# GpSimd waits for VectorE operations on two SBUF inputs, more time for the first loads in the event model, and other seeds for the order

## The chip, the cores and the metric

The kernel runs on one core of one Trainium2 chip. The metric is device time in microseconds (us) of one execution. Two kernels are compared by the medians of several runs; a single further execution is taken with the hardware profiler, and all rows of the profile come from that one.

The core has five engines that run their own instruction streams and meet at semaphores: TensorE (PE in the profile; its weight loads are shown apart as PEld), VectorE (DVE), ScalarE (ACT), GpSimd (POOL) and SyncE (SP), which here issues nearly all DMAs. Each engine takes its instructions strictly in the order in which the program wrote them.

## The reference, cut to what matters

The kernel computes a block and all of its gradients: out = g · A(x) + (1 − g) · B(x), with 2048 rows of 512 columns in bf16.

```
qkv = (x @ wqkv)                    # 32 heads of 16 columns
scores = q @ k.T * 16 ** -0.5       # masked: 0 <= i - j < 256
a = softmax(scores) @ v @ wo        # A: attention in a sliding window of 256
gate = x @ W_gate; up = x @ W_up    # 512 -> 1376
b = (relu(gate) * up) @ W_down      # B
g = sigmoid((x * gate_w).sum(-1))
out = g * a + (1 - g) * b
_out, _vjp = jax.vjp(f, x, wqkv, wo, W_gate, W_up, W_down, gate_w)
return (_out, *_vjp(grad_out))
```

So there are eight outputs: the block's output, and the gradients of x, wqkv, wo, W_gate, W_up, W_down and gate_w.

## The kernel before

**Tiles and stages.** Attention is cut into 32 stages of four heads by 512 rows. A stage has score products (S) and products of the output gradient with V (dP), both made by the matmuls of line L1101 in a "row" mode, in which four matmuls with 16 or 32 rows of weights share the array. ScalarE takes the exponential of S out of PSUM (L1144), GpSimd masks the triangles at the edges of the window (L1122), and VectorE multiplies the masked result by dP (L1149). The sums over keys and queries are matmuls of line L1165 in a "col" mode, with 32 columns of weights each. Everything else on TensorE is "dense": projections, feed-forward layers and weight gradients go through one helper (L698), the products that give the output and the gradient of x through another (L1472).

**The feed-forward layer.** `front` handles one of eleven chunks of 128 hidden columns. For every 512 rows it makes three products by matmul, takes a relu on ScalarE or VectorE (L936, L938), then multiplies on VectorE (L941, L945). Two more products have both inputs in SBUF (L948); they may go to GpSimd or to VectorE. A chunk's results go to DRAM by a DMA and come back transposed.

**The order of the work.** No loop of the program issues instructions directly. The program first lists operations (`op`, `dma`), each with the engines that may run it, a cost in nanoseconds for each, a rank, and the buffers it reads and writes. Then `Flow.run` walks through a small event model: whenever an engine of the model is free, it takes the ready operation with the lowest rank, emits its instructions, and marks the engine as taken for the stated cost. So the model's costs fix both the order within each engine's stream and which engine gets an operation that two could run. On the chip the order is kept, and semaphores do the waiting; the model's times are not enforced.

**Lock operations.** Operations that may run on VectorE with their inputs in SBUF alone carry `lock=True`: L948, the products U and pr of a stage (L1196, L1198), the copies at L1034 and L1036, the scaling of the output gradient by the gate (L877), and in the last part the small sums of `dzf` (L1572, L1573, L1607, L1608) and the running sum of `gate_sum` (L1540). In the model VectorE starts such an operation only while GpSimd is free, and GpSimd starts nothing until it has ended (`locked`). That rule lives in the model alone: the emitted program has no semaphore for it.

**DMAs in the model.** All DMAs that SP and ACT issue share one line of time (`dma_free`), with a cost by bytes. An operation that would start a DMA of rank 3 or more is held back while that line is over 1500 ns ahead. `load_first` brings the first rows and weights, and `load_rows` then loads the other rows of x and of the output gradient, three loads of 512 KB each. The first stage of attention needs the arrays `QD_d` and `KV_d`, which the first projections write to DRAM (L838), and reads them back (L1024 to L1026).

**Seeds.** Among dense matmul operations the rank gets a small pseudo-random addition. Its seed and its size come from the list `SEEDS`, one entry for every 20,000 ns (`STRETCH`) of the model's time, and the last entry holds for all that follows:

```python
s_ = SEEDS[min(int(now / STRETCH), len(SEEDS) - 1)]
return o.rank + SPREADS[s_ % len(SPREADS)] * mix(s_ // len(SPREADS), o.seq)
```

TensorE's mode counts in the model too: changing between row, col and dense costs 97 ns (`SWITCH`), and an addition of 2.5 to the rank (`HOLD`) puts off a change from dense to col for up to 800 ns. When TensorE has nothing to do and has lately been idle, the model inserts a matmul into a free bank (L1638) that nobody reads.

**The last part.** After the attention stages come the products of L1472 for the output and the gradient of x. There `final` adds, on GpSimd, two partial results that come back from DRAM (L1577, L1582), and stores them.

Of the kernel before, what the change touches and what calls it, by code (L numbers as in the profile page):

```python
# [34 lines left out]
def place(segs, dist):  # L35
# [13 lines left out]
PE, DVE, ACTE, POOL, SP = "PE", "DVE", "ACT", "POOL", "SP"  # L49
START = 20000  # L50
LATENCY = {PE: 230, DVE: 135, ACTE: 165, POOL: 100, SP: 2300}
# [2 lines left out]
HOLD, WAIT = 2.5, 800  # L54
SPREADS, STRETCH = (0.05, 0.15, 0.02, 0.4), 20000
SEEDS = (
# [3 lines left out]
)  # L60
SPAN, LOW, NEED, PHASE = 3413.3, 3000, 3600, 0

# [154 lines left out]
class Flow:  # L217
# [6 lines left out]

    def __init__(self):
        self.ops, self.spare, self.fill, self.filled = [], None, None, 0

    def op(self, times, fn, r=(), w=(), order=(), deps=(), keep=(), rank=5, mode="", nbytes=0, heavy=False,
           lead=0, lock=False):
# [45 lines left out]
    def run(self):  # L275
        events, count = [], 0
        ready = {e: [] for e in LATENCY}
        free = {e: 0.0 for e in LATENCY}
        now, dma_free, pool_free, locked, mode, heavy, done = 0.0, 0.0, 0.0, 0.0, "", False, 0
        self.log, self.busy, self.slow, ran = [], [], {}, {}  # L280

# [42 lines left out]
        while done < len(self.ops):  # L324
            progress = True
            while progress:
                progress = False
                for e in (PE, ACTE, DVE, POOL, SP):
# [24 lines left out]
                    else:  # L353
                        o = min(cands, key=lambda o: (o.rank, o.seq))
# [6 lines left out]
                    if e == PE:  # L361
                        took = ahead(now + SWITCH * (o.mode != mode), took)
                        if o.mode != mode:
                            took += SWITCH
                        mode = o.mode
                        if o.mode == "den":
                            heavy = o.heavy
                    o.fn(e)
                    o.state = 1
                    self.log.append((now, took, e, o))  # L370
                    free[e] = now + took
# [40 lines left out]
def kernel(  # L412
# [41 lines left out]
    WARM = 4  # L454
    MASKV = {DVE: 410, ACTE: 710}
    DTT = 640
    TT = 425
    KR = 2.5
    HQ, OUTS, DIRECT = (SP,), 2, 3
# [197 lines left out]
        rings[nm].ordered = True  # L657

    fl = Flow()
    op = fl.op  # L660
    EN = {PE: nc.tensor, ACTE: nc.scalar, DVE: nc.vector, POOL: nc.gpsimd, SP: nc.sync}

# [79 lines left out]
    def load_rows(dst, src_d, sb, on=(SP,)):  # L742
        dma(lambda q: q.dma_start(dst[:, 4 * sb:4 * sb + 4, :],
                                  src_d[sb * W:(sb + 1) * W, :].rearrange("(t p) d -> p t d", p=P)),
            w=[(dst, sb)], nbytes=512 * KB, rank=2 if on == by_pool else 3, on=on)

    def load_first():

# [918 lines left out]
```

## Time and profile before

| what | value |
|---|---|
| median of 3 runs | 802.11 us (800.44 to 804.85) |
| profiled execution: its own time | 803.82 us |
| profiled execution: span of its instructions | 802.1 us |
| mean granted TensorE clock | 0.998 |
| bytes read from HBM, written to it | 55.02 MB, 55.74 MB |

The span runs from the first to the last instruction in the trace; about 1.7 us of the execution's own time lie around it. How to read rows of the groups: the line in the program, the engine, the operation, what it writes and reads, the shape, the count; behind the bar the busy time in us and the mean duration of one in ns; behind the second bar the idle time of the engine just before, and whose end released it. Busy intervals of successive instructions on an engine overlap a little, since one begins while the one before drains.

### The profile page before, as it was taken

The page shows a single profiled execution, that of the slowest core. Times are in us where ns is not written, and L with a number is a line of the kernel's source. Part 1 is how long each engine was busy: PE and PEld are TensorE (multiplying, and loading weights), DVE is VectorE, ACT ScalarE, POOL GpSimd, SP SyncE. Part 2 cuts the span into 40 slices and gives each one's busy share as a digit, 9 for nine tenths or more (in the row PEclk, how much of TensorE's full clock was granted, in tenths as well). Part 3 has the DMA queues.
Part 4 walks back from the last instruction along what each step waited for, and adds up shares of the span by engine and source line. Part 5 has one row for each costly group of instructions (what it writes and reads, how often), then busy time and mean ns, then how long its engine had stood idle before and what let it go on. Part 6 is the DMA issues. An engine that isn't in the chain of part 4 may idle for free.

```text
span 802.1 us, 24151 instructions
## 1 busy us (share of the span) xinstructions
PE 782.5 (98%) x8842; PEld 371.0 (46%) x8950; DVE 696.6 (87%) x1239; ACT 589.1 (73%) x1183; POOL 546.8 (68%) x972
## 2 busy tenths in 40 slices
PE   8899999999999999999999999999999999999999
PEld 5443444445445454444454554544443434344444
DVE  3589999999999999999999988998999999933573
ACT  4786889888888778887888998888877888421121
POOL 2497879787797988797988676776766666222145
PEclk9999999999999999999999999999999999999999
DMA  9879657478679999997899979686745685497896
GB/s 239 183 178 222 154 135 185 113 175 181 130 189 163 233 178 188 231 208 220 189 202 210 212 157 204 161 193 182 221 108 173 160 246 173 141 272 223 230 236 191
DMA packets 313009, 152.18 MB, mean 190 GB/s; under 512 B 203161, under 2 KB 303194, under 8 KB 312250
## 3 DMA queue, kind: packets, MB, share of 16 engines
q1 hardware_dynamic: 311314, 148.53, 77.0%
q0 software_dynamic: 496, 1.44, 0.9%
q8 instruction: 70, 1.15, 0.6%
q10 hardware_dynamic: 1080, 0.66, 0.3%
q14 instruction: 49, 0.40, 0.2%
HBM read 55.02 MB, written 55.74 MB: 138 GB/s over the span
## 4 chain that ended last, share of the span: by engine, by line
PE 91%; DMA 3%; issue 2%; DVE 2%; ACT 1%; SPq 1%; ACTq 0%; DVEq 0%
PE banks L698 42%; PE banks L1472 21%; PE banks L1101 15%; PE banks L1165 10%; DMA arena<-in_A_x_dram 1%; DVE arena L1149 1%; PE banks L1200 1%; ACT arena L1144 1%; DMA arena<-QD_d 1%; DMA arena<-HD_d 1%; PE banks L802 1%; DMA arena<-wt_d 0%; PE banks L1638 0%; SPq L1006 0%; SPq L768 0%
## 5 line engine op out<-in xcount | busy, mean ns | idle before, releaser
L1149 DVE TENSOR_TENSOR arena<-arena,banks 128x512 bf16<-128x512 bf16 (+1 forms) x740 | 455.8, 665 | 20.5 <-PE banks L1101 12.8
L1144 ACT ACTIVATE arena<-banks 128x512 bf16<-128x512 f32 (+1 forms) x740 | 394.3, 588 | 80.3 <-PE banks L1101 61.0
L1122 POOL TENSOR_SCALAR_AFFINE_SELECT arena<-arena 128x256 bf16<-128x256 bf16 (+1 forms) x752 | 345.4, 483 | 142.6 <-ACT arena L1144 132.8
L698 PE MATMUL banks<-arena 128*128 128x512 bf16 (+4 forms) x1929 | 385.5, 334 | 5.5 <-issue 1.6
L698 PEld LDWEIGHTS <-arena 128*128 128x128 bf16 (+1 forms) x2000 | 175.1, 98 | 154.9 <-issue 54.5
L1472 PE MATMUL banks<-arena 128*128 128x512 bf16 (+1 forms) x747 | 181.8, 380 | 3.2 <-issue 1.9
L1101 PE MATMUL banks<-arena 32*128 32x128 bf16 (+5 forms) x2944 | 155.8, 271 | 5.5 <-DMA arena<-QD_d 2.0
L1101 PEld LDWEIGHTS <-arena 32*128 32x128 bf16 (+1 forms) x2944 | 47.9, 92 | 140.3 <-issue 136.3
L1472 PEld LDWEIGHTS <-arena 128*128 128x128 bf16 (+1 forms) x784 | 69.6, 98 | 89.8 <-issue 17.4
L676 ACT CAST arena<-banks 128x512 bf16<-128x512 f32 (+4 forms) x150 | 71.4, 489 | 44.9 <-PE banks L698 35.2
L1165 PE MATMUL banks<-arena 128*32 128x128 bf16 (+5 forms) x2944 | 92.2, 271 | 0.4 <-DVE arena L1149 0.2
L948 POOL TENSOR_TENSOR arena<-arena 128x512 bf16<-128x512 bf16 (+1 forms) x73 | 84.1, 1156 | 3.4 <-ACT arena L676 2.1
L1165 PEld LDWEIGHTS <-arena 128*32 128x32 bf16 (+1 forms) x2944 | 61.2, 95 | 30.8 <-issue 18.2
L1196 POOL TENSOR_TENSOR arena<-arena 128x512 bf16<-128x512 f32 x31 | 35.9, 1158 | 16.1 <-issue 12.4
L1576 ACT ACTIVATE arena<-banks,g_all 128x512 f32<-128x512 f32 x12 | 8.2, 687 | 42.8 <-PE banks L1472 28.4
L678 DVE CAST arena<-banks 128x512 bf16<-128x512 f32 (+3 forms) x50 | 31.0, 625 | 9.5 <-PE banks L698 7.2
L1577 POOL TENSOR_TENSOR arena<-arena 128x512 bf16<-128x512 f32 x12 | 15.3, 1276 | 29.5 <-ACT arena L1576 12.1
L1198 POOL TENSOR_TENSOR arena<-arena 128x512 bf16<-128x512 bf16 x29 | 33.4, 1153 | 0.8 <-DVE arena L1196 0.7
L1582 POOL TENSOR_TENSOR arena<-arena 128x512 bf16<-128x512 f32 x12 | 15.2, 1265 | 25.9 <-DMA arena<-dx_p 14.4
L941 DVE SCALAR_TENSOR_TENSOR arena<-arena,banks 128x512 bf16<-128x512 bf16 (+1 forms) x44 | 29.9, 679 | 0.6 <-PE banks L698 0.2
L945 DVE TENSOR_TENSOR arena<-arena,banks 128x512 bf16<-128x512 bf16 (+1 forms) x44 | 29.8, 676 | 0.0
L1567 DVE SCALAR_TENSOR_TENSOR arena<-banks,g_all,arena 128x512 bf16<-128x512 f32 x12 | 8.8, 748 | 23.6 <-ACT arena L1576 23.6
(95 smaller groups left out, 421.6 us busy)
## 6 DMA issues: line engine op xcount, KB each, us to landing
ffn_d<-arena SPq DMA_DIRECT2D x40, 384.0 KB
arena<-ffn_d SPq DMA_DIRECT2D x88, 128.0 KB
out_dram<-arena SPq DMA_DIRECT2D x66, 128.0 KB
arena<-HD_d SPq DMA_DIRECT2D x32, 256.0 KB
KV_d<-arena SPq DMA_DIRECT2D x32, 128.0 KB
QD_d<-arena SPq DMA_DIRECT2D x32, 128.0 KB
arena<-KV_d SPq DMA_DIRECT2D x32, 128.0 KB
arena<-QD_d SPq DMA_DIRECT2D x32, 128.0 KB
```

The lines of the kernel that those rows point to most:

```text
L676: nc.scalar.copy(out, in_)
L678: EN[e].tensor_copy(out, in_)
L698: return lambda start, stop: nc.tensor.matmul(out_fn(), lhsT=lhs_fn(), rhs=rhs_fn(), start=start, stop=stop)
L948: op({POOL: t_pool(W, 2), DVE: TT}, lambda e, q=q, k=k, b=b: EN[e].tensor_tensor(out=q["act"][:fs, k, :], in0=q["dhs"][:fs, :], in1=q[b][: ...
L1101: nc.tensor.matmul(bank, lhsT=lt[rs, ls], rhs=rt[rs, rsl], start=True, stop=True)
L1122: nc.gpsimd.affine_select(out=v, in_=v, compare_op=ALU.is_ge, fill=0.0, base=0 if kind == "D" else -1, pattern=[[0, 2], [0, cnt], [sgn, P] ...
L1144: op({ACTE: t_act(u.width)}, lambda e, u=u, b=b, bank_=bank_: nc.scalar.activation(part(u, u.Pt, b), bank_[:, :u.width], ACT.Exp), r=[bank ...
L1149: op({DVE: t_dve(u.width)}, lambda e, u=u, b=b, bank_=bank_: nc.vector.tensor_tensor(out=part(u, u.Pd, b), in0=part(u, u.Pt, b), in1=bank_ ...
L1165: nc.tensor.matmul(acc[32 * i:32 * i + wt.shape[1], q0:q0 + cnt * P], lhsT=wt, rhs=m[:, i % 2, col * P:(col + cnt) * P], start=(k == 0), s ...
L1196: op({POOL: t_pool(W, 2), DVE: t_dve(W)}, lambda e: EN[e].tensor_tensor(out=U[:], in0=ri[:], in1=qd[:], op=ALU.mult), r=[ri, qd], w=[U], r ...
L1198: op({POOL: t_pool(W, 2), DVE: TT}, lambda e: EN[e].tensor_tensor(out=pr[:], in0=OB[:, half], in1=U[:], op=ALU.mult), r=[(OB, half), U], w ...
L1472: nc.tensor.matmul(bank[:], lhsT=l_(), rhs=r_(), start=(lo + k == 0), stop=(lo + k == n - 1))
```

## The change

Three things are changed.

1. A real dependency. When the model emits a lock operation on VectorE, its last instruction is remembered. The next operation emitted for GpSimd that is no DMA gets a semaphore dependency on it: its first instruction waits until the VectorE instruction has ended. One GpSimd operation per remembered instruction waits; if two lock operations come before it, it waits for the later one. The costs in the model stay as they are.
2. The model's account of the start. SP and ScalarE are taken as busy for the first 800 ns, and the six loads of `load_rows` count as 1.2 times their bytes in the model. The transfers themselves are the same.
3. Other seeds. The 40 entries of `SEEDS` are replaced by 41 others. Both lists end in 0.

```diff
 SEEDS = (
-    16914, 36512, 34193, 28631, 17467, 29116, 12171, 23200, 15639, 5432, 22622, 33577, 13710, 2535, 15625, 10269,
...
-    33217, 31493, 2658, 18911, 29376, 22502, 20490, 0,
+    27601, 11357, 7558, 39987, 14011, 590, 1533, 1815, 15419, 11593, 7005, 28378, 21291, 5427, 32748, 20263,
...
+    23287, 31690, 18602, 19721, 10719, 36758, 32196, 39551, 0,
 )
...
+        self.held, self.traced, self.after = None, None, None
...
-        free = {e: 0.0 for e in LATENCY}
+        free = {e: 800.0 if e in (SP, ACTE) else 0.0 for e in LATENCY}
...
+                    made = self.traced()
+                    count_ = len(made)
                     o.fn(e)
+                    made = [i for i in made[count_:]]
+                    if e == DVE and o.lock:
+                        self.held = made[-1]
+                    elif e == POOL and self.held is not None and not o.nbytes:
+                        self.after(made[0], self.held)
+                        self.held = None
...
+    EARLY_X = 1.2
...
+    def after(inst, first):
+        tc.add_manual_dep(inst, first.name, mybir.DependencyInfo(mybir.DependencyClass.Sync, mybir.DependencyReason.DATA), reason="port")
+
+    fl.traced, fl.after = lambda: nc.cur_bb.bb.instructions, after
...
-            w=[(dst, sb)], nbytes=512 * KB, rank=2 if on == by_pool else 3, on=on)
+            w=[(dst, sb)], nbytes=EARLY_X * 512 * KB, rank=2 if on == by_pool else 3, on=on)
```

Since the whole stream comes out of one walk through the model, items 2 and 3 can alter the order of nearly every instruction and the engine of every operation that has a choice. The amount of arithmetic stays the same.

2 rows, old and new, of the table SEEDS are left out of this document.

## The prediction

> **What bounds the kernel now.** The page comes first: span, busy times, and the chain that ended last.
>
> ```profile
> span 802.1 us, 24151 instructions
> PE 782.5 (98%) x8842; PEld 371.0 (46%) x8950; DVE 696.6 (87%) x1239; ACT 589.1 (73%) x1183; POOL 546.8 (68%) x972
> PE 91%; DMA 3%; issue 2%; DVE 2%; ACT 1%; SPq 1%; ACTq 0%; DVEq 0%
> ```
>
> TensorE is busy for 98% of the span and is 91% of the chain. All its idle time is 802.1 − 782.5 = 19.6 us. That is the most that removing visible waits can win, so the next view asks where it lies: busy times of four stretches (start, first attention stage, middle, last part).
>
> ```profile
> 0.00:32.00 32.00, 26.02 (x273) 17.51 (x278) 14.03 (x41) 16.93 (x33) 8.51 (x24) 0.99 0.97 236
> 32.00:40.00 8.00, 7.95 (x57) 3.52 (x55) 5.25 (x8) 6.05 (x14) 5.28 (x14) 0.81 0.44 110
> 40.00:700.00 660.00, 648.32 (x8007) 303.45 (x8100) 628.04 (x1079) 547.05 (x1095) 501.22 (x910) 1.00 0.78 182
> 700.00:802.10 102.10, 100.25 (x512) 46.49 (x519) 49.30 (x114) 19.06 (x43) 31.80 (x25) 1.00 0.85 230
> ```
>
> The columns are length, then busy time of PE, PEld, DVE, ACT and POOL, granted clock, DMA share, GB/s. TensorE idles 6.0 us before 32 us, 11.7 us between 40 and 700 us, and 1.9 us after that. The granted clock falls to 0.81 between 32 and 40 us. VectorE is nearly full in the middle as well (628 of 660 us), so what it loses there is not easily made up; GpSimd has 159 us left.
>
> The waits then say who is late (us in total, times, longest); all engines first, then TensorE's own.
>
> ```profile
> PEld L1101 <- issue: 136.3, 375, 2.4
> POOL arena L1122 <- ACT arena L1144: 132.8, 181, 9.2
> PEld L698 <- issue: 54.5, 255, 0.7
> PEld L1165 <- issue: 18.2, 72, 0.4
> PEld L1472 <- issue: 17.4, 83, 0.2
> ```
> ```profile
> PE banks L1101 <- DMA arena<-QD_d: 2.0, 1, 2.0
> PE banks L698 <- DVE arena L1149: 0.9, 2, 0.7
> PE banks L1101 <- DVE arena L1149: 0.5, 2, 0.3
> ```
>
> Two things are to be seen. TensorE's named waits are few: one DMA in front (2.0 us), and VectorE's L1149 (0.9 + 0.5 us). And there are 785 gaps in the weight loads that have no releaser, 226 us in all: they come where TensorE changes between row, col and dense work. They do not count as idle, because the matmuls before them still drain, but they are why an order with fewer changes is shorter with the same arithmetic.
>
> **Part one, the wait on GpSimd.** What it removes is in VectorE's and GpSimd's groups.
>
> ```profile
> L1149 DVE TENSOR_TENSOR arena<-arena,banks 128x512 bf16<-128x512 bf16 x704 | 443.7, 679 | 19.3 <-PE banks L1101 11.7 <-issue 3.9 <-ACT arena L676 0.3
> L948 DVE TENSOR_TENSOR arena<-arena 128x512 bf16<-128x512 bf16 x14 | 11.4, 822 | 0.2 <-ACT arena L676 0.2
> L948 DVE TENSOR_TENSOR arena<-arena 96x512 bf16<-96x512 bf16 x1 | 1.6, 1600 | 0.0
> L1572 DVE TENSOR_TENSOR arena<-arena,sb_all 128x1 f32<-128x1 f32 x12 | 5.8, 485 | 0.2
> ```
>
> The product L948 takes VectorE 822 ns on average, and one took 1600 ns with fewer rows. The timeline shows what a short one and two long ones look like:
>
> ```profile
> 327.38 0.46 DVE L948 TENSOR_TENSOR arena<-arena 128x512 bf16<-128x512 bf16 x1
> ...
> 307.83 1.15 POOL L948 TENSOR_TENSOR arena<-arena 128x512 bf16<-128x512 bf16 x1
> 307.91 1.35 DVE L948 TENSOR_TENSOR arena<-arena 128x512 bf16<-128x512 bf16 x1
> ...
> 310.24 0.39 PE L1101 MATMUL banks<-arena 16*128 16x384 bf16 x6 [0.28 <-DVE arena L1149]
> ...
> 57.85 0.80 POOL L850 DMA_DIRECT2D wi_d<-arena  x1
> 57.98 2.14 DVE L948 TENSOR_TENSOR arena<-arena 128x512 bf16<-128x512 bf16 x1
> 58.67 1.17 POOL L948 TENSOR_TENSOR arena<-arena 128x512 bf16<-128x512 bf16 x1
> 60.78 0.59 PE L698 MATMUL banks<-arena 128*128 128x512 bf16 x2 [0.74 <-DVE arena L1149]
> ```
>
> At 307.91 VectorE began 0.08 us behind GpSimd's 1.15 us product and ended 0.28 us after it. At 57.98 it stood through the rest of a DMA issue and all of a GpSimd product that began 0.69 us later than itself. So VectorE stands while GpSimd works. In both places L1149 is late next, and TensorE waits for it: 0.28 and 0.74 us.
>
> With 0.46 us as the undisturbed time, the excess is 14 × (0.822 − 0.46) + (1.60 − 0.46) = 6.2 us of VectorE. This bounds the gain from above. From below it is nothing: the wait holds back only a GpSimd operation that follows in the order and comes early; one that precedes and is late still holds VectorE. I take what TensorE's waits on L1149 show, 0.9 + 0.5 = **1.4 us**, since TensorE sets the end.
>
> The Trainium skill, page "SBUF — State Buffer", section "Who interferes with whom", says that a VectorE operation with two SBUF inputs contends with GpSimd operations that read SBUF, but infers that it leaves the writing of DMA descriptors alone. The start at 57.98 differs from that: alone it would have ended at 58.44, before 58.67, yet it ended at 60.12, so the DMA issue held it as well. The new wait spares DMAs; by the trace about a third of that one stand (0.7 us of 1.7) would stay, by the page none, which moves the sum by 0.3 us at most.
>
> What it adds: about 24 waits between 40 and 700 us (VectorE ran 15 of L948 and about nine of the smaller ones there). Each holds GpSimd by up to the 0.46 us that VectorE needs, 24 × 0.46 = 11 us. Behind the waiting instruction queue the masks L1122, for which L1149 and the sums L1165 wait. The cover is GpSimd's 159 us of idle time there, most of it spent waiting for ScalarE's L1144 (132.8 us). I take nothing, and keep 0 to 11 us as the bounds. In the last part the lock operations (L1572 among them, 485 ns with one element per row) precede GpSimd's additions, whose stores end the program:
>
> ```profile
> 796.15 1.27 POOL L1582 TENSOR_TENSOR arena<-arena 128x512 bf16<-128x512 f32 x1 [0.68 <-DMA arena<-dx_p]
> ...
> 799.73 0.27 SPq L1633 DMA_DIRECT2D out_dram<-arena  x1
> ```
>
> The last addition ends at 797.42, 2.3 us ahead of the last store's issue. This hides single waits of about 0.5 us; nothing.
>
> **Part two, the first loads.** They are issued by the model's order; no byte goes away. The stall that a truer account could move:
>
> ```profile
> 25.57 0.46 SPq L1025 DMA_DIRECT2D arena<-QD_d  x1
> ...
> 31.48 0.59 PE L1101 MATMUL banks<-arena 16*128 16x384 bf16 x8 [1.96 <-DMA arena<-QD_d]
> ```
> ```profile
> 31.00:32.00 1.00, 0.52 (x8) 0.15 (x9) 0.00 (x0) 0.00 (x0) 0.00 (x0) 0.79 1.41 311
> 32.00:33.00 1.00, 1.00 (x7) 0.43 (x4) 0.00 (x0) 0.96 (x2) 0.00 (x0) 0.50 0.88 200
> 33.00:34.00 1.00, 1.00 (x6) 0.47 (x4) 0.07 (x1) 1.00 (x4) 0.80 (x3) 0.50 0.23 34
> 34.00:35.00 1.00, 1.00 (x11) 0.61 (x9) 0.77 (x2) 0.80 (x2) 1.00 (x4) 0.51 0.71 223
> ```
>
> The read of QD_d took 5.9 us from issue to use, and the first row matmul stood for it 1.96 us. Right behind, the clock was at half for 3.4 us, which costs 0.21 + 0.50 + 0.50 + 0.49 = 1.7 us of TensorE's work. Best case: the model now expects the DMA later, puts dense matmuls in front, and both go: −3.7 us. Worst: the walk finds a front that stalls once more like this, +3.7 us. I take all of the wait and half of the clock, 1.96 + 0.85 = **2.8 us**, because dense work was at hand (other L698 matmuls follow at once), while no row shows by what rule the clock falls. Whatever is saved in front must pass the middle; TensorE is full there, so it arrives at the end whole.
>
> The Trainium skill, page "TensorE: Matmul & The Clock Gate", section "What's actually happening", puts the half clock behind a whole idle window of about 3.4 us. Here a gap of 1.96 us preceded it, so the trace differs. By the page that gap would not be the cause, the 0.85 us would fall out, and the sum would be higher by as much.
>
> **Part three, other seeds.** The arithmetic is the same; the number of changes is not. A change costs 54.5 / 255 = 0.21 us ahead of dense loads and 136.3 / 375 = 0.36 us ahead of row loads. Ten changes more or less in 785 are 2 to 4 us. I know no row that says which way; I take 0, with ±5 us (about 20 changes of the mean 226 / 785 = 0.29 us). The list being one entry longer is at most a weak hint that the planned order is longer.
>
> **Sum.** Against the profiled execution: 803.82 − 1.4 − 2.8 ± 0 = 799.6 us. That execution lay 803.82 − 802.11 = 1.7 us over the median, so on the median's scale 802.11 − 4.2 = 797.9, rounded to **798 us**; its own range is 794 to 801.5.
>
> **The rivals.**
>
> *The order has more changes: slower.* Place: between 40 and 700 us, in TensorE's changes of mode. With 30 changes more (4%) it loses 30 × 0.29 = 8.7 us, and 802.1 − 4.2 + 8.7 = 806.6 us. It decides from 15 changes more, where it eats the 4.2 us. For it speaks that these gaps are more than ten times the idle time, so small differences in the walk weigh more than both mended places. Against it: the ranks, `SWITCH` and `HOLD`, which keep modes together, are unchanged.
>
> *GpSimd's waits reach the masks: slower.* If two thirds of the 11 us (7.3) come through to L1149 and L1165, the contention is only exchanged for this wait: 802.1 − 2.8 + 7.3 = 806.6 us. It decides from 2.8 us coming through. Against it speaks GpSimd's idle time ahead of L1122.
>
> *Nothing net.* VectorE is held as before, because the GpSimd operations that hold it precede it, or the dependency yields no wait; the front stalls elsewhere. Time 802 us. For it: only 1.4 us of TensorE's waits are tied to L1149.
>
> *The order has fewer changes: faster still.* Twenty fewer give 798 − 5.8 = 792 us.
>
> **How the numbers follow.** Forecast 0.41, more changes 0.20, waits on the masks 0.08, nothing net 0.16, fewer changes 0.15. A measurement of this kernel can tell about 0.5% (4 us) from no change, so faster means under 798.1 and slower over 806.1. Of the forecast's 0.41, 0.24 lie under that bound and 0.17 within; fewer changes is all faster (0.15); nothing net puts 0.14 within and 0.02 slower; the two slower rivals put 0.02 within and 0.26 slower. That is 0.39 faster, 0.33 within, 0.28 slower. The range runs from 791 (just past the fewer changes) to 808 (just past the two slower cases).
>
> **What would show it.** The wait: DVE L948 near 0.46 us instead of 0.82, L1572 near 0.16, no wait of TensorE on L1149 behind an L948; GpSimd's idle time ahead of L1122 and L948 with VectorE as a releaser, under 11 us. The front: no stall on QD_d near 30 us and a clock of 1.00 between 31 and 35 us. The order: the count of gaps in the weight loads near 785. The prediction is wrong if the gaps grow by 15 or more, if L1149 waits for masks, or if the first 40 us keep 6 us of idle time.

## The result and the profile after

| kernel | median, us | lowest to highest | runs |
|---|---|---|---|
| before | 801.57 | 800.44 to 804.85 | 5 |
| changed | 796.29 | 795.86 to 797.83 | 5 |

The ratio is 0.9936, with a 95% interval of 0.9914 to 0.9958: the changed kernel is 5.3 us faster. A second comparison with other runs (told below) gave 0.9944, 0.9924 to 0.9963. The profiled execution took 797.83 us, 1.7 us of them around its span.

The page of the changed kernel, its span, busy times and chain:

```profile
span 796.1 us, 24191 instructions
PE 780.9 (98%) x8843; PEld 370.1 (46%) x8950; DVE 686.8 (86%) x1241; ACT 590.7 (74%) x1183; POOL 546.3 (69%) x970
PE 93%; DMA 2%; issue 2%; DVE 2%; ACT 1%; POOL 0%; SPq 0%; DVEq 0%; ACTq 0%; POOLq 0%
```

The same four stretches of the changed kernel (length, then busy time of PE, PEld, DVE, ACT and POOL, granted clock, DMA share, GB/s):

```profile
0.00:32.00 32.00, 28.82 (x277) 19.14 (x281) 13.78 (x41) 18.90 (x37) 9.31 (x25) 1.00 0.87 230
32.00:40.00 8.00, 7.36 (x62) 2.84 (x62) 4.64 (x9) 6.18 (x16) 4.30 (x12) 1.00 0.92 167
40.00:700.00 660.00, 650.35 (x8061) 304.06 (x8156) 625.12 (x1089) 547.31 (x1091) 500.70 (x909) 1.00 0.78 184
700.00:796.10 96.10, 94.35 (x456) 44.05 (x457) 43.29 (x104) 18.31 (x41) 31.98 (x25) 1.00 0.84 231
```

TensorE idles 3.2 us before 32 us (6.0 before the change), 0.6 between 32 and 40 (0.05), 9.7 between 40 and 700 (11.7) and 1.8 behind (1.9). Both traces lack the records of over 100 matmuls (8843 here, 8842 before, beside 8950 weight loads), so these figures are upper bounds. The clock is full throughout, and VectorE is busy 9.8 us less in all.

Where the 6.0 us between the two spans lie is seen from the row matmuls. The first fence is the view of L1101 in the kernel before, the second that of the same line, now L1116, in the changed one; behind the count stand the shortest, median and longest duration in ns, then the first and the last start, which bound the attention stages.

```profile
L1101 PEld LDWEIGHTS <-arena x2944: 90/91/113, 31.4 to 703.1; 16*128 16x128 bf16 x99, 32*128 32x128 bf16 x98
```
```profile
L1116 PEld LDWEIGHTS <-arena x2944: 89/92/95, 32.3 to 697.1; 16*128 16x128 bf16 x99, 32*128 32x128 bf16 x98
```

The first row matmul comes 0.9 us later than before. From there to the last it is 664.8 us instead of 671.7, and from the last to the end 99.0 us in both. So the whole gain, and 0.9 us more, lies inside the attention stages. Of these 6.9 us, 1.7 are the half clock that the profiled execution of before had between 31 and 35 us; most executions lack it.

The waits of the changed kernel, TensorE's matmuls, its weight loads, and GpSimd's masks (us, times, longest):

```profile
...
PE banks L1116 <- ACT arena L1159: 0.5, 1, 0.5
PE banks L713 <- DVE arena L1164: 0.4, 2, 0.2
```
```profile
PEld L1116 <- issue: 133.0, 374, 0.4
PEld L713 <- issue: 56.8, 266, 0.8
PEld L1180 <- issue: 17.5, 72, 0.4
PEld L1487 <- issue: 17.0, 81, 0.2
```
```profile
POOL arena L1137 <- DVE arena L1051: 2.6, 2, 1.3
POOL arena L1137 <- DVE arena L963: 2.4, 5, 0.8
POOL arena L1137 <- DVE arena L1049: 1.3, 3, 0.7
POOL arena L1137 <- ACT arena L1159: 121.5, 163, 9.0
```

The wait for QD_d is gone, and 0.4 us are left on the multiplication by dP (L1149 before, L1164 now) where 1.4 were. The gaps in the weight loads are now 793, eight more than before, though their sum is 224.3 us instead of 226.4. The new waits show as VectorE releasing the masks: 2.6 + 2.4 + 1.3 = 6.3 us. VectorE's groups of the changed kernel:

```profile
L1164 DVE TENSOR_TENSOR arena<-arena,banks 128x512 bf16<-128x512 bf16 x704 | 445.4, 680 | 20.5 <-PE banks L1116 13.4 <-issue 1.0 <-POOL arena L1137 0.8
L963 DVE TENSOR_TENSOR arena<-arena 128x512 bf16<-128x512 bf16 x12 | 5.4, 468 | 0.0
L963 DVE TENSOR_TENSOR arena<-arena 96x512 bf16<-96x512 bf16 x1 | 0.6, 595 | 0.0
L1587 DVE TENSOR_TENSOR arena<-arena,sb_all 128x1 f32<-128x1 f32 x12 | 2.8, 230 | 0.1
```

The product (L948 before, L963 now) went from 822 to 468 ns, the small sums (L1572, now L1587) from 485 to 230 ns. L1164 waits 0.8 us for masks in all (0.5 us in the same order without the wait, told below): what GpSimd now waits for VectorE hardly reaches VectorE again.

### The profile page after: what moved, and what is told of

It reads as the page before. It is cut to its first block, busy times and chain, and to the rows that moved or that the text cites. A ratio compares the mean times of both kernels' runs of the same rounds, so it can differ in the third digit from the quotient of the medians.

```text
span 796.1 us, 24191 instructions
## 1 busy us (share of the span) xinstructions
PE 780.9 (98%) x8843; PEld 370.1 (46%) x8950; DVE 686.8 (86%) x1241; ACT 590.7 (74%) x1183; POOL 546.3 (69%) x970
## 3 DMA queue, kind: packets, MB, share of 16 engines
q8 instruction: 70, 1.15, 0.6%
## 4 chain that ended last, share of the span: by engine, by line
PE 93%; DMA 2%; issue 2%; DVE 2%; ACT 1%; POOL 0%; SPq 0%; DVEq 0%; ACTq 0%; POOLq 0%
PE banks L713 43%; PE banks L1487 22%; PE banks L1116 15%; PE banks L1180 11%; PE banks L817 1%; PE banks L1215 1%; DVE arena L1164 1%; DMA arena<-KV_d 1%; DMA arena<-in_A_x_dram 0%; DMA arena<-in_A_wo_dram 0%; DMA out_dram<-arena 0%; ACT arena L1159 0%; DVE arena L1209 0%; PE banks L1653 0%; PE banks L793 0%
## 5 line engine op out<-in xcount | busy, mean ns | idle before, releaser
L1164 DVE TENSOR_TENSOR arena<-arena,banks 128x512 bf16<-128x512 bf16 (+1 forms) x740 | 457.2, 665 | 21.2 <-PE banks L1116 13.8
L1116 PE MATMUL banks<-arena 32*128 32x128 bf16 (+5 forms) x2944 | 154.0, 270 | 2.3 <-ACT arena L1159 0.5
L1116 PEld LDWEIGHTS <-arena 32*128 32x128 bf16 (+1 forms) x2944 | 47.2, 92 | 136.3 <-issue 133.0
L691 ACT CAST arena<-banks 128x512 bf16<-128x512 f32 (+5 forms) x154 | 74.9, 499 | 41.5 <-PE banks L713 31.2
L963 POOL TENSOR_TENSOR arena<-arena 128x512 bf16<-128x512 bf16 (+1 forms) x75 | 86.2, 1156 | 4.4 <-ACT arena L691 1.6
L1592 POOL TENSOR_TENSOR arena<-arena 128x512 bf16<-128x512 f32 x12 | 15.2, 1265 | 44.9 <-DMA arena<-b_d 23.4
L693 DVE CAST arena<-banks 128x512 bf16<-128x512 f32 (+3 forms) x46 | 26.6, 585 | 2.9 <-PE banks L713 1.2
L1400 ACT ACTIVATE arena<-arena,ez_all 128x128 bf16<-128x128 bf16 x64 | 20.6, 412 | 9.6 <-DMA arena<-HD_d 9.6
```

The costliest lines, as they stand in the source:

```text
L691: nc.scalar.copy(out, in_)
L963: op({POOL: t_pool(W, 2), DVE: TT}, lambda e, q=q, k=k, b=b: EN[e].tensor_tensor(out=q["act"][:fs, k, :], in0=q["dhs"][:fs, :], in1=q[b][: ...
L1116: nc.tensor.matmul(bank, lhsT=lt[rs, ls], rhs=rt[rs, rsl], start=True, stop=True)
L1164: op({DVE: t_dve(u.width)}, lambda e, u=u, b=b, bank_=bank_: nc.vector.tensor_tensor(out=part(u, u.Pd, b), in0=part(u, u.Pt, b), in1=bank_ ...
```

## The experiments

Each ratio is against the kernel before on the same chip. The account of the first loads, the seeds and the wait can be switched separately, and each experiment is one such switching or a probe of one price. The new seeds with the old account of the start were not run.

**The wait alone, in the order of before.** The model's account of the start and the seeds stay those of before, so the streams are those of before plus semaphores.

```diff
+                    if e == DVE and o.lock:
+                        self.held = made[-1]
+                    elif e == POOL and self.held is not None and not o.nbytes:
+                        self.after(made[0], self.held)
+                        self.held = None
```

> The kernel before with the new semaphore wait and nothing else: each engine keeps the instruction order of before. My theory (the wait is worth what TensorE loses to a late L1149, 1.4 us): 801.6 - 1.4 = 800.2 us, ratio 0.998, with VectorE's L948 near 0.46 us instead of 0.82. Rival one (the order and the front did all of it, the wait only moves the stand from VectorE to GpSimd): 801.6 us, ratio 1.000, L948 short all the same. Rival two (VectorE is nearly full, so all of its 6.2 us of excess reach the end): 795.5 us, ratio 0.992. Rival three (the waits hold back the masks): over 803 us.

Measured: 796.9 us against 801.31, ratio 0.9952 (0.9933 to 0.9971). So the wait is worth 3.8 us by the ratio in this order, close to three times the price that I gave it. VectorE's product is as short as in the changed kernel (last row below). But the larger surprise is in front. The timeline of the kernel before, then of this one (start and duration in us, engine, line, operation; in brackets how long the engine stood before, and whose end released it):

```profile
21.44 0.61 POOL L844 COPY arena<-arena 128x512 bf16<-128x512 bf16 x1
...
22.55 0.75 POOL L725 DMA_DIRECT2D arena<-in_A_wqkv_dram  x1
23.29 0.76 POOL L850 DMA_DIRECT2D wi_d<-arena  x1
...
25.57 0.46 SPq L1025 DMA_DIRECT2D arena<-QD_d  x1
```
```profile
25.01 1.10 SPq L1040 DMA_DIRECT2D arena<-QD_d  x1
25.44 0.61 POOL L859 COPY arena<-arena 128x512 bf16<-128x512 bf16 x1 [4.00 <-DVE arena L892]
...
26.56 0.75 POOL L740 DMA_DIRECT2D arena<-in_A_wqkv_dram  x1
27.30 0.76 POOL L865 DMA_DIRECT2D wi_d<-arena  x1
...
29.43 0.40 PE L1116 MATMUL banks<-arena 16*128 16x384 bf16 x8
```
```profile
L963 DVE TENSOR_TENSOR arena<-arena 128x512 bf16<-128x512 bf16 x14 | 6.4, 464 | 0.2 <-ACT arena L691 0.2
```

GpSimd's copy waits 4.00 us for VectorE's scaling of the output gradient (L877 before, L892 now). Two DMAs stand behind it in GpSimd's queue, and so start 4.0 us later, after the read of QD_d has been issued instead of ahead of it. The first row matmul then starts at 29.43 without a wait, where it stood 1.96 us and started at 31.48. So the stall on QD_d went with the wait alone, in an order whose loads were not touched.

**The new order without its wait.**

```diff
-                        self.after(made[0], self.held)
+                        pass
```

> The changed kernel without the semaphore wait: its instruction order, its account of the start and its seeds stay. My theory: the wait's 1.4 us are lost again, 796.3 + 1.4 = 797.7 us, ratio to before 0.995, and VectorE's product on two SBUF inputs goes back to about 0.8 us on average. Order only: 796.3 us, ratio 0.9935. All of VectorE's excess counts: above 801 us, ratio 0.999 or more.

Measured: 796.56 us, ratio 0.9946 (0.993 to 0.9962). The new order alone is worth as much as the whole change. It has few of the collisions in it to begin with: its twelve products take 526 ns on average without any wait, against 822 in the order of before.

```profile
L963 DVE TENSOR_TENSOR arena<-arena 128x512 bf16<-128x512 bf16 x12 | 6.1, 526 | 0.0
```

Of the stall on QD_d it keeps 0.4 us.

**The changed kernel once more, and its wait behind the front alone.** The second applies the wait only where the model's time is 30 us or more:

```diff
-                        self.after(made[0], self.held)
+                        if now >= 30000:
+                            self.after(made[0], self.held)
```

> The changed kernel once more, on the same chip and beside the same runs of the kernel before as the three others: 796.3 us, ratio 0.9936 within its interval. It shows whether the wait in the old order (796.9 us in the first runs) and the whole change differ by more than the measurement can tell; I expect them equal within 1.5 us.

> The changed kernel with the wait emitted only from 30 us of the model's time on, so that GpSimd's copies and DMAs in front run early. In the new order the front does not depend on them (QD_d is read at 28 us, with dense work ahead of its first use), so the time stays at 796.3 us, ratio 0.994. If the front's wait helps in this order as in the old one, it is 798 us; if it hurts, 795 us.

Measured: 796.52 us, ratio 0.9944 (0.9924 to 0.9963), and 796.5 us, ratio 0.9941 (0.992 to 0.9961). In the new order, then, the medians with no wait at all (on another chip), with waits behind the front only and with all waits differ by 0.06 us, the ratios by 0.0005, or 0.4 us. The intervals reach 1.3 to 1.6 us to each side, so a worth of a microsecond can't be excluded here; 3.8 us can.

**The wait in the order of before, split at 30 us of the model's time.** The same condition, once as "below 30000" and once as "from 30000 on".

> The old order with the wait emitted only for the three GpSimd operations that the model starts before 30 us (the copy L1034, the copy L844 in front of GpSimd's five DMAs, and the first mask). New theory: the wait alone won 4.4 us in two halves. In front it puts off GpSimd's DMAs past the read of QD_d, so the first row matmul starts near 29.4 us instead of 31.3 (-2 us); in the middle it ends the stands of VectorE (-2 us). Then this kernel takes 799.3 us, ratio 0.9975, its first row matmul starts at 29.4 us and L948 still takes 0.82 us. Rival: the early first row matmul was chance or comes from elsewhere; then 801.3 us, ratio 1.000, and it starts near 31.3.

> The old order with the wait emitted only from 30 us of the model's time on (35 waits). New theory: the front stays as before (first row matmul near 31.3 us), VectorE's L948 falls to 0.46 us, and the middle wins 2 us: 799.2 us, ratio 0.9975. Rival: all of the 4.4 us come from VectorE's stands: 796.9 us, ratio 0.9945. Other rival: all from the front: 801.3 us, ratio 1.000.

Measured: front alone 799.4 us, ratio 0.998 (0.9965 to 0.9996), and the rest alone 797.58 us, ratio 0.9966 (0.9946 to 0.9986). By the ratios that is 1.6 and 2.7 us of 801, together 4.3, which agrees within the intervals with the 3.8 of both. The intervals are wide: 0.3 to 2.8 us for the front, 1.1 to 4.3 for the rest. With the front alone, VectorE's product keeps its 808 ns, and the row matmuls begin at 28.9 us; with the rest alone it takes 462 ns, and the stages between the first and the last row matmul take 666.4 us, where they take 670.5 with the front alone. The two effects are separate.

**Is the half clock behind the stall worth anything?** Nine matmuls that nobody reads are put in front of the first row matmul of the kernel before, which keeps TensorE at work while it waits for QD_d.

```diff
+                    if e == PE and o.mode == "row" and not self.kept_warm:
+                        self.kept_warm = True
+                        for _ in range(9):
+                            self.fill(self.spare.free[-1])
```

> The kernel before with nine matmuls of 512 columns put on TensorE just ahead of the first row matmul, into a free bank that nobody reads; the order of all else stays. They take 9 x 0.216 = 1.9 us, about the 1.96 us that TensorE stood there for the read of QD_d. If that idle time is what halves the clock behind it, the clock stays at 1.00 between 31 and 35 us and up to 1.7 us are won: 799.9 us, ratio 0.998. If the half clock has another cause it stays, and the time is 801.6 us, or longer by what the fillers run past the landing (up to 0.5 us). The stall on the DMA itself is not won by either theory.

Measured: 801.94 us against 801.31, ratio 1.0008 (0.9997 to 1.0018): nothing. In this comparison no execution of the kernel before had a clock below 1.000, so there was nothing to win, and whether the idle time causes the half clock stays untested. In the 57 executions of the kernel before in the experiments the mean clock was 0.996 to 0.998 in 11; they took 803.0 to 806.2 us, the other 46 799.2 to 802.9. On the two chips where both kinds came up, the medians of the two kinds lie 4.0 and 3.5 us apart. The profiled execution of before (0.998, 803.82 us) was of the rarer kind, while the median is not.

This trace also has a record for every matmul (8959 weight loads and as many matmuls), while those of before and after lack 108 and 107. Its page, for the order of before:

```profile
PE 792.9 (99%) x8959; PEld 371.6 (46%) x8959; DVE 697.0 (87%) x1239; ACT 588.9 (73%) x1183; POOL 547.1 (68%) x972
```

With a span of 801.6 us TensorE idles 8.7 us; the nine inserted matmuls fill another 2.0 (from 29.15 to 31.19 us), so without them it would be some 10.8, not 19.6. Much of the idle time that the prediction counted was missing records.

**The account of the start with the old seeds, without and with the wait.** A third order, which nobody chose: the model's walk starts differently, and the seeds were picked for another walk.

```diff
-        free = {e: 0.0 for e in LATENCY}
+        free = {e: 800.0 if e in (SP, ACTE) else 0.0 for e in LATENCY}
...
-            w=[(dst, sb)], nbytes=512 * KB, rank=2 if on == by_pool else 3, on=on)
+            w=[(dst, sb)], nbytes=EARLY_X * 512 * KB, rank=2 if on == by_pool else 3, on=on)
```

> The kernel before with the new account of the start alone (800 ns for SP and ScalarE, six loads at 1.2 times their bytes), with the old seeds and no wait. If the account is worth its 2.8 us with any seeds, the time is 798.8 us, ratio 0.9965. If the seeds fit only the model in which they were sought, the whole order behind the front is a random one, and the time is longer than before by 10 to 25 us, ratio 1.012 to 1.031, although the front itself is free of the stall on QD_d.

> The old seeds with the new account of the start, a third order that took 816.5 us without the wait, now with the wait. In that run VectorE's L963 took 699 ns on average (old order 822, new order 526). Theory: the wait is worth what collisions an order happens to have, times a common rate. The old order won 2.7 us behind the front for (0.822 - 0.46) x 14 + 1.14 = 6.2 us of excess; this one has (0.699 - 0.46) x 17 = 4.1 us, so 1.8 us there; its front has dense work ahead of the first row matmul, so nothing there: 814.7 us, ratio to before 1.0170. Rival: the wait's worth is tied to the tuned old order alone: 816.5 us, ratio 1.0190.

Measured: 816.49 us, ratio 1.0196 (1.0175 to 1.0216), without the wait, and 814.51 us, ratio 1.0146 (1.0117 to 1.0176), with it. By the ratios the wait is worth 4.0 us here, with intervals that touch; the two medians, which come from different chips, are 2.0 us apart. The ratios flatter it: beside the run with the wait, seven of the 17 executions of before had the half clock, and against the median of the other ten (801.19 us) it would be 1.0166, which leaves 2.4 us. And all four executions without the wait had a mean clock of 0.998, while four of the seven with it had 1.000, so a part of the difference may be the clock's. The last part of the third order without the wait, behind its last row matmul at 704.4 us, beside that of the kernel before (behind 703.1), and the inserted matmuls of the third order:

```profile
704.40:815.00 110.60, 107.72 (x548) 49.76 (x547) 46.92 (x107) 20.27 (x44) 33.41 (x26) 1.00 0.82 226
```
```profile
703.10:802.10 99.00, 97.30 (x495) 45.53 (x503) 46.20 (x108) 18.99 (x42) 31.80 (x25) 1.00 0.85 230
```
```profile
L1653 PE MATMUL banks<-arena,ident 128*128 128x512 bf16 x24 | 6.7, 378 | 1.3 <-DVE arena L1582 1.0 <-DVE arena L1164 0.2
```

There are 24 inserted matmuls, where the order of before with the wait has eight, all at the end. Fifteen of the 24 lie beside attention, from 483 us on: there the model itself ran out of dense work. Its last part takes 110.6 us instead of 99.0, with 44 more weight loads in it (547 against 503). Dense work that found no place beside attention was left for the end, when little is there to run with it. Its gaps in the weight loads are 799 in all (385 + 261 + 78 + 75), only 14 more than before; at 0.29 us each that is 4 of the 15 us, and by their measured sum (231.5 us, 226.4 before) it is 5.

The middle of four kernels whose traces have all records: order of before (with the nine inserted matmuls), order of before with the wait, new order without the wait, third order.

```profile
40.00:700.00 660.00, 656.01 (x8082) 302.95 (x8077) 628.48 (x1078) 545.51 (x1091) 500.05 (x907) 1.00 0.78 182
```
```profile
40.00:700.00 660.00, 657.57 (x8097) 303.24 (x8099) 625.05 (x1082) 545.00 (x1090) 496.84 (x905) 1.00 0.78 184
```
```profile
40.00:700.00 660.00, 659.11 (x8138) 303.99 (x8137) 624.95 (x1087) 546.83 (x1090) 502.32 (x905) 1.00 0.78 185
```
```profile
40.00:700.00 660.00, 653.08 (x8042) 301.24 (x8044) 618.10 (x1067) 547.47 (x1096) 498.35 (x907) 1.00 0.76 178
```

The matmuls that pass in these 660 us, 8082, 8097, 8138 and 8042, stand in the order of the four spans (801.6, 796.8, 794.4 and 815.0 us), and so does TensorE's idle time there: 4.0, 2.4, 0.9 and 6.9 us.

**The price of a collision by itself.** A small kernel leaves out the whole computation and only runs operations of VectorE and GpSimd alone and beside each other.

> A kernel of its own that leaves out the whole computation: ScalarE writes a tile, and its end releases one operation on VectorE and one on GpSimd, six times for each pair, 128x512 bf16 throughout. Alone: VectorE's product of two SBUF tiles 0.42 us, GpSimd's product 1.15 us, its mask 0.64 us, its DMA issue 0.75 us. If VectorE stands while GpSimd holds SBUF, then the product beside GpSimd's product takes VectorE up to 1.15 + 0.42 = 1.6 us when GpSimd begins first, or GpSimd is stretched when VectorE begins first; with one input in PSUM nothing happens (0.68 us). The disputed case is a DMA issue on GpSimd: by the timeline at 58 us of the kernel before it holds VectorE, about 0.75 + 0.42 = 1.2 us; by the Trainium skill's inference (SBUF - State Buffer, Who interferes with whom) it does not, 0.42 us.

Its timeline, in five cases: VectorE's product alone, GpSimd's product alone, GpSimd's product when VectorE's began 0.05 us ahead of it, GpSimd's product beside a VectorE product with one input in PSUM, and VectorE's product when a mask of GpSimd began 0.11 us ahead of it.

```profile
4.66 0.43 DVE L39 TENSOR_TENSOR dv<-go,y 128x512 bf16<-128x512 bf16 x1 [0.68 <-ACT go L36]
...
12.13 1.15 POOL L48 TENSOR_TENSOR po<-go,y 128x512 bf16<-128x512 bf16 x1 [0.73 <-ACT go L36]
...
49.71 1.39 POOL L48 TENSOR_TENSOR po<-go,y 128x512 bf16<-128x512 bf16 x1 [0.73 <-ACT go L36]
...
89.92 1.15 POOL L48 TENSOR_TENSOR po<-go,y 128x512 bf16<-128x512 bf16 x1 [0.73 <-ACT go L36]
...
117.86 0.61 POOL L51 TENSOR_SCALAR_AFFINE_SELECT po<-go 128x512 bf16<-128x512 bf16 x1 [1.05 <-ACT go L36]
117.97 0.79 DVE L39 TENSOR_TENSOR dv<-go,y 128x512 bf16<-128x512 bf16 x1
```

In these cases whoever begins later pays. GpSimd behind VectorE loses 0.24 us of the 0.42 that VectorE needs. VectorE behind a mask takes 0.79 us instead of 0.42 and ends at 118.76, 0.29 us behind the mask (118.47). With one input in PSUM there is no collision. A copy of VectorE (one input, in SBUF) that begins first stretches GpSimd's product a little, to 1.25 us. An issue of a DMA beside VectorE's product changed nothing, but VectorE had always begun first there.

**An issue of a DMA that begins first.** A second kernel of this kind, which also leaves out the whole computation, repeats the stand at 57.98 us in the profile of before.

> This kernel leaves out the whole computation; it only puts small VectorE operations on PSUM in front, so that VectorE's 128x512 product of two SBUF inputs begins while an instruction of GpSimd is already under way. Five series, four times each: a DMA issue of GpSimd alone (128x4x256 bf16 out of SBUF); the VectorE product begun shortly behind such an issue; the same with a GpSimd product queued right behind the issue, which is the situation at 57.98 us of the profile of before; the VectorE product begun behind the first of two GpSimd products in a row; and behind a mask that a GpSimd product follows. The theory (the issue holds VectorE as computing does, and VectorE waits for everything that GpSimd has in a row): VectorE takes over 0.42 us behind an issue alone, about 0.9 us; about 2.1 us where a product follows the issue; and about 2.2 us behind two products. The rival (the issue does not hold VectorE; the 2.14 us came of the GpSimd product behind it and of the VectorE products ahead): 0.42 us behind an issue alone, and behind an issue with a product 0.42 us as well if VectorE is first at the lock, and GpSimd's product is stretched by 0.24 us. Of the two products in a row: if VectorE comes in between them, it takes about 1.3 us, and if not, about 2.2 us.

Its timeline: VectorE's product begun 0.39 us into an issue; the same with a GpSimd product behind the issue; and behind the first of two GpSimd products in a row (these two are one row).

```profile
26.44 0.75 POOL L61 DMA_DIRECT2D wide_d<-wide  x1 [2.40 <-ACT wide L40]
26.83 0.42 DVE L43 TENSOR_TENSOR dv<-go,y 128x512 bf16<-128x512 bf16 x1
...
29.98 1.91 DVE L43 TENSOR_TENSOR dv<-go,y 128x512 bf16<-128x512 bf16 x1
30.44 1.17 POOL L52 TENSOR_TENSOR po<-go,y 128x512 bf16<-128x512 bf16 x1
...
43.41 2.44 POOL L52 TENSOR_TENSOR po<-go,y 128x512 bf16<-128x512 bf16 x2 [1.09 <-ACT go L39]
...
43.78 1.06 DVE L43 TENSOR_TENSOR dv<-go,y 128x512 bf16<-128x512 bf16 x1
```

An issue alone does not hold VectorE: 0.42 us, as when alone. Behind an issue with a product in its wake VectorE takes 1.91 us and ends 0.28 us after that product (31.89 against 31.61), though the product's record begins 0.46 us after VectorE's. This is the stand of 57.98, made at will. Between two products VectorE does come in: it ends at 44.84, 0.28 us after the first one would end (43.41 + 1.15). Between a mask and a product it comes in as well (0.52 us, ending 0.29 us behind the mask). Why a product behind an issue goes ahead of a VectorE operation that is already recorded as begun, no row here shows.

In the order of before with the wait, the same three instructions as at 57.85 stand in its timeline like this:

```profile
54.54 0.80 POOL L865 DMA_DIRECT2D wi_d<-arena  x1
54.66 0.42 DVE L963 TENSOR_TENSOR arena<-arena 128x512 bf16<-128x512 bf16 x1
...
55.36 1.17 POOL L963 TENSOR_TENSOR arena<-arena 128x512 bf16<-128x512 bf16 x1
```

The issue is as before and VectorE begins 0.12 us into it, but the product behind the issue has a wait on VectorE: 2.14 us have become 0.42, and GpSimd's product begins 0.02 us after the end of the issue (55.34).

The Trainium skill, page "SBUF — State Buffer", section "Who interferes with whom", gives the order of issue as what decides who is held, and infers that a VectorE operation of this kind leaves the writing of DMA descriptors alone. The 0.42 us beside a lone issue agrees with the second. The 1.91 us, where VectorE's record begins 0.46 us ahead of the product's, doesn't agree with the first, if the records' starts are the order of issue; an issue with a product behind it the page doesn't treat.

**An attempt to be faster.** In the order of before with the wait, one stand of TensorE is left that has a clear cause: at 481 us it waits 1.14 us for ScalarE, which is held by its scaling by exp(z), whose data come late. Here that scaling is emitted six ScalarE operations later in three of four column blocks.

```diff
+            z = op({ACTE: 4 * t_scale(P)}, by_z, r=[(RW, sb), wsets["gate"][sb]], w=[(Or, sb)], rank=2)
+            z.defer = 6 if c < 3 else 0
```

> The old order with the wait, and with ScalarE's scaling by exp(z) (four instructions for each 512 rows, for three of the four column blocks) emitted six ScalarE operations later, everything else in its place. In the old order TensorE still stood 1.1 us near 481 us, because ScalarE stood 1.9 us at such a scaling for the read of HD_d with L1159 queued behind it. If that stand is what is left, 796.9 - 1.5 = 795.4 us, ratio 0.9935, which is below the changed kernel's 796.4; if the stand only moves to the next late DMA, 796.9 us, ratio 0.9952.

Measured: 802.48 us, ratio 0.9999 (0.9984 to 1.0015): the whole gain of the wait is lost. At that place TensorE now waits 0.57 us, but its waits as a whole read

```profile
PE banks L1126 <- ACT arena L1169: 2.0, 5, 0.8
...
PE banks L723 <- ACT arena L1169: 0.9, 1, 0.9
```

(L1169 is the exponential, L1144 before): as I read it, the deferred scaling pushes other exponentials back. In the kernel with the wait alone the same two waits are 1.1 and 0.7 us, so these 2.9 us are only 1.1 more. The loss against the wait alone is 3.8 us by the ratios (5.6 by the medians of two chips); what makes up the rest wasn't found. No version that ran is clearly faster than the changed kernel.

## Why the prediction was right, and where it was not

Direction and size were right (798 forecast, 796.29 measured), but the sum came out right by terms that were not: one was too small, one had a part without a basis, and one counted the wrong thing. That they added up to nearly the measured time is luck.

**The wait, 1.4 us forecast.** The mechanism was right where I saw it: the product went from 822 to 468 ns (464 in the old order), near the 0.46 us named, though the small sums stayed at 230 ns instead of some 160. The size was too small: in the old order the wait is worth 3.8 us (2.3 to 5.4). Behind the front it is 2.7, whose interval (1.1 to 4.3) still holds 1.4. I counted only stands in which TensorE's wait names L1149 as the last releaser; that the 6.2 us of VectorE's excess reach TensorE by other ways too is likely, but not shown. And one path was missed altogether. I listed the masks as what queues behind GpSimd's waits, and did not count the DMAs that queue there too; in front it is two of them, and holding them back by 4.0 us removes the stall on QD_d, 1.6 us by the ratio. That the later DMAs are the cause is read from their place in the timeline; a kernel that moves these DMAs alone wasn't tried.

**How much of this is in the change.** In the new order the wait is worth nothing that can be measured (796.56 without it; with it 796.29 in the first comparison, 796.52 in the second). So the two parts do not add. The order of before with the wait reaches 796.9, the new order alone 796.56, both together 796.3 to 796.5. Three traces that have all matmul records, one execution each, show where the two overlap. The table has TensorE's idle time ahead of the first row matmul, from there to the last, and behind it (length of the stretch less busy time).

| kernel | front, us | stages, us | last part, us |
|---|---|---|---|
| order of before, its nine inserted matmuls counted as idle | 4.9 | 4.0 | 1.9 |
| order of before with the wait | 2.8 | 2.5 | 1.1 |
| new order without the wait | 2.9 | 1.3 | 1.2 |

Either part by itself takes out about 2 us in front, 1.5 or 2.7 in the stages and 0.7 behind them, and as I read it, what one has taken is no longer there for the other. The collisions fit: by the prediction's own sum VectorE's excess is 6.2 us in the order of before and 0.9 in the new one without the wait. That the wait has a worth of its own, apart from the order, was a hidden assumption of my sum.

**The first loads, 2.8 us forecast.** As named, the stall on QD_d is gone and the clock is full. Not all of that is the account's doing: in the new order without the wait 0.4 us of the stall are left, and with the wait behind the front only 0.8. The row matmuls begin 0.9 us later than before, and the gain lies in the stages behind; what TensorE no longer idles in front (6.0 − 3.2 = 2.8 us) went into other matmuls done earlier (287 weight loads ahead of the first row matmul instead of 269, 8168 instead of 8180 in the stages). The half clock (0.85 us of the 2.8) had no basis: it is found in 11 of 57 executions, the profiled one among them, and not in a typical one. The median contains none of it, and the step that set the sum against one execution and then shifted it to the median carried it over.

**Other seeds, 0 ± 5 us by the count of changes.** This step failed as a method. The gaps rose from 785 to 793, and the kernel became faster; in the third order they rose to 799, and it lost 15 us, of which the gaps themselves explain about 5. Between the new order without the wait (785 gaps) and the third order (799) the count differs by 14, or 4 us at 0.29 us each, while the gaps' sum differs by 9.5 us (222.0 and 231.5). Seeds alone, with the account of the start kept, are worth 816.49 − 796.56 = 19.9 us, four times my bound. As far as the traces show, what separates the orders is how much dense work finds a place beside attention (24 inserted matmuls and a last part of 110.6 us in the bad one), and how long TensorE idles there (4.0, 2.4, 0.9, 6.9 us). Both can be read from a trace, neither from the count of changes. The account of the start alone is no gain but a loss of 15.2 us, as long as the seeds are not matched to it.

**What bounds the kernel.** "All its idle time is 19.6 us" was too high, since 108 of 8950 matmuls had no record; the complete trace of that order shows some 10.8 us (8.7 with the nine inserted matmuls at work). The row that would have told it stood in the prediction: 8842 matmuls beside 8950 weight loads.

**The rivals.** "More changes" came true in its count and not in its price. "Waits reach the masks" is refuted as a price: masks wait 6.3 us for VectorE, and VectorE waits 0.8 us for masks, where 2.8 would have decided. That L1149 waits for masks at all was named as a sign of being wrong; it came, but 0.5 of the 0.8 us stand in the same order without the wait. "Nothing net" is refuted by the interval. "Fewer changes, 792" did not happen.

**The DMA issue as a holder of VectorE.** My reading of 57.98 us, that the issue held the product, was wrong; the product queued behind the issue did. The new wait, which skips DMAs and goes to that product, thus leaves nothing of that stand (2.14 us became 0.42), where I let a third of it stay by the trace.

## What to carry to other kernels

A wait that is added to an engine holds everything in that engine's queue, its DMAs too: list these first, since a DMA that leaves 4 us later can be worth as much as the collision that the wait was made for. Price two remedies for the same loss together and not as a sum, and test each without the other. Before a term is taken from a single profiled execution, see whether its clock is that of the other runs and whether its matmul records are as many as its weight loads.

## What the runs showed of the hardware that was not expected

- A VectorE product of two SBUF inputs that is held ends 0.28 to 0.29 us after the GpSimd operation that holds it, in each of the cases read: 307.91 and 57.98 us in the profile of before, and in the small kernels a mask, a product, and a product behind an issue.
- A GpSimd product behind a DMA issue goes ahead of a VectorE product recorded as begun 0.46 us earlier (VectorE 1.91 us), while between two GpSimd products VectorE comes in (1.06 us).
- Collisions belong to the order and not to chance: the mean of VectorE's product in the order of before is 822 ns in one execution, 824 with the nine inserted matmuls and 808 with the wait in front alone; in the changed kernel it is 468 and 448 ns in two executions.
- A mean clock below 1.000 is found in 11 of 57 executions of the kernel before, in none of one comparison's 17 and in 7 of another's 17; where it lies is seen in the profiled one alone, behind the stall of 1.96 us. The third order had it in all four executions, in its trace at half from about 547 to 550 us, and TensorE had idled only 1.4 us in all between 540 and 547. The Trainium skill, page "TensorE: Matmul & The Clock Gate", section "What's actually happening", says that the window in which activity is watched runs free, so that its effect varies from run to run; that fits the counts of the kernel before. It names an idle window of about 3.4 us, longer than the idle time in either place, which no run here explains.
